# A gated MLP's output projection: float16 weights with scales, and gated rows transposed through DRAM

## The chip, the core and the metric

The kernel runs on one core of a Trainium2 chip. A core has five engines that work side by side, each through its own instructions in order: PE (TensorE, matrix products and transposes, into PSUM), ACT (ScalarE), DVE (VectorE), POOL (GpSimd) and SP (SyncE, which here only issues DMAs). They hand work to each other through semaphores. The metric is the device time of one execution in microseconds (us). The kernel before takes 1732.87 us, median of three runs (1732.65 to 1733.68).

## The reference

A transformer block with pre-normalisation: attention with 32 heads of 16 on 2048 rows of 512, and then a gated MLP whose gate mixes rows.

```python
def _A_ref(x, wqkv, wo):          # 32 heads, Dh = 16
    qkv = (x @ wqkv).reshape(B, S, 3, H, Dh)...
    p = softmax(einsum("bhqd,bhkd->bhqk", q, k) * Dh ** -0.5)
    o = einsum("bhqk,bhkd->bhqd", p, v)
    return o.reshape(B, S, D) @ wo

def _B_ref(x, w_in, w_sp, b_sp, w_out):
    z = gelu(x @ w_in)            # 2048 x 1376
    z1 = z[..., :688]
    z2 = layernorm(z[..., 688:])
    g = einsum("ts,bsf->btf", w_sp, z2) + b_sp[None, :, None]
    return (z1 * g) @ w_out       # 688 -> 512

h = x + _A_ref(layernorm(x), wqkv, wo)
out = h + _B_ref(layernorm(h), w_in, w_sp, b_sp, w_out)
```

Everything is float32 in DRAM. The kernel keeps about float32 accuracy by splitting an operand into a float16 (or float32r) high part and the low part that remains, and by making each product of three: high times high, high times low, low times high (`mm3`, L107 to L110).

## The kernel before

Four stages follow each other. The **projections** (to about 160 us) make q, k and v. **Attention** (to 1296) goes over pairs of key blocks; ACT makes the exponentials, PE scores and weighted sums, DVE maxima. In its shadow POOL does chores: it splits w_sp's quarters, w_in, wo and, last, w_out in six pieces (`out_piece`, through `job`, a planner that deals the chores out by their estimated times), scaled by `out_down` and stored to DRAM as float32r parts (`wu_scr`). Toward the end of attention the first row blocks of its output are fetched (`load_o`), scaled on POOL and split (`split_o`: ACT's cast at L735, DVE's low part at L736) by the iteration numbers n.

The **middle stage** (1296 to 1455) takes 16 row blocks, k = 0 to 15. For a row block PE makes h (`make_h`), transposes the normalised rows (`turn`: PE, a cast on ACT at L99, a low part on DVE at L105), and makes z in four quarters (`make_z`: 12 float16 matmuls of 128x344 into PSUM each, gelu on ACT at L1206). `gate_z` normalises z2, writes z1 to DRAM and forms the sums and differences b11, t1, t2, b22, t3, b21, n4 of the quarters of z2, each cast to float16 (L1210) with a low part (L1211) by `parts`. They feed a Strassen-like product with seven products in the place of eight.

The **final stage** (from 1455.2) runs over p = 0 to 7, a pair of row blocks (p and p + 8) each. `product` (24 float16 matmuls of 128x344, 3.5 us) is called seven times, for b11, t1, t2, b22, t3, b21, n4, into three PSUM banks A, C, B; operands of w_sp's parts come by DMA into a ring of nine (`ask`). ACT evicts p1, q5 and v (L1397, L1402, L1407), DVE adds the four halves right, br, left, bl of the gated rows (L1412 to L1426), POOL multiplies three of them by z1. Between the products of pair p stand the steps of pair p − 1, in a class `Out`: `turn` transposes a gated row block on PE (six 128x128 transposes into PSUM, L1327), `split` casts on ACT (L1335) and takes low parts on DVE (L1336, L1339), `multiply` does 17 float32 matmuls of 128x512 with w_out's parts `wu`, and `store` adds h and writes out (L1357, L1358). `fetch` (L1368) loads z1 and h of the next pair on SP.

The program asks for a manual schedule in the last two stages: every engine issues in the order of the text, and so does SP with its DMAs. Tiles are freed and given out by pools; a tile of a new pool waits for the last access of the closed pools whose memory it takes.

Of the kernel before, what the change touches and what calls it, by code (L numbers as in the profile page):

```python
# [8 lines left out]
F32 = mybir.dt.float32  # L9
# [31 lines left out]
FB = [(i * P, min(P, FH - i * P)) for i in range(6)]  # L41
# [18 lines left out]
def block_kernel(ctx: ExitStack, tc: tile.TileContext, x, wqkv, wo, w_in, w_sp4, b_sp, w_out, out):  # L60
# [30 lines left out]
    wu_scr = [dram.tile([P, 2, D], F32, name=f"wu{i}_scr") for i in range(len(FB))]  # L91
# [640 lines left out]
    def split_o(sb):  # L732
        o = os_.pop(sb)
        o2s[sb] = [e2.tile([P, DB, P], F16, name=f"o2{i}", bufs=1) for i in range(2)]
        nc.scalar.activation(o2s[sb][0], o, AF.Copy, scale=o_up)  # L735
        nc.vector.scalar_tensor_tensor(o2s[sb][1], o, o_up, o2s[sb][0], op0=ALU.mult, op1=ALU.subtract)  # L736
# [47 lines left out]
    with ExitStack() as at:  # L784
# [181 lines left out]
        def out_piece(i):  # L966

            f0, n = FB[i]
            got, load = piece(w_out[f0:f0 + n, :], n)
            t = []  # L970

            def high():
                t.append(wp.tile([P, 2, D], F32R, name="wup", bufs=4)[:n])
                pool.tensor_copy(t[0][:, 0], got[0])

            def low():
                pool.tensor_sub(t[0][:, 1], got[0], t[0][:, 0].bitcast(F32))

            job(load, [(lambda: times(got[0], out_down), TS), (high, CAST), (low, TT)], 12)
            soon(len(chores) + LATER, lambda: nc.sync.dma_start(wu_scr[i][:n], t[0].bitcast(F32)))  # L980

# [69 lines left out]
        for i in range(len(FB)):  # L1051
            out_piece(i)
# [6 lines left out]
        for n in range(0, len(units), 2):  # L1059
# [120 lines left out]
    with ExitStack() as mid:  # L1180
# [28 lines left out]
        def parts(name, k, src, eh, el):  # L1209
            (nc.gpsimd.tensor_copy if eh == "pool" else nc.scalar.copy)(T[name][0][:, k, :], src)  # L1210
            (nc.gpsimd if el == "pool" else nc.vector).tensor_sub(T[name][1][:, k, :], src, T[name][0][:, k, :])  # L1211

        def gate_z(sb, meanwhile):
# [26 lines left out]
            parts("b22", k, b22, "act", el)  # L1240
            nc.gpsimd.tensor_sub(b12, b22, b12)
            parts("t3", k, b12, "pool", "pool")
            parts("b21", k, b21, "act", None)
            e.tensor_sub(t2, b21, t2)
            parts("n4", k, t2, eh, el)

        row = dict(enumerate(h_rows))
        with tc.manual_schedule(engines={E.PE, E.Activation, E.DVE, E.Pool, E.SP}):
# [3 lines left out]
            for k in range(NB):  # L1252
# [38 lines left out]
    with ExitStack() as fin:  # L1291
# [4 lines left out]
        ps_g = fin.enter_context(tc.tile_pool(name="fin_g", bufs=4, space=PSUM))  # L1296
        WB = len(FB) - 1
        TW = P // 2
        fn = FB[-1][1]
# [9 lines left out]
        class Out:  # L1309


            def __init__(self, tb, h, pr):
                self.rows, self.h, self.pr = slice(tb * P, (tb + 1) * P), h, pr
                self.pT = self.acc = None

            def turn(self, *halves):

                if self.pT is None:
                    self.pT = [f2.tile([P, WB + 1, P], F32R, name="pT0"),
                               f2.tile([P, WB, P], F32R, name="pT1")]  # L1320
                    self.tps = {}
                for half in halves:
                    i0 = 3 * half
                    tp = self.tps[half] = ps_t.tile([P, 4, P], F32, name="tp")
                    for i in range(i0, i0 + 3):
                        c = i * P if i < WB else FH - TW
                        nc.tensor.transpose(tp[:, i - i0, :], self.pr[:, c:c + P], ident)  # L1327

            def split(self, *halves):

                hi, lo = self.pT
                for half in halves:
                    i0, tp = 3 * half, self.tps.pop(half)
                    n = 3 - half
                    nc.scalar.activation(hi[:, i0:i0 + 3, :], tp[:, :3, :], AF.Copy)  # L1335
                    nc.vector.tensor_sub(lo[:, i0:i0 + n, :], tp[:, :n, :], hi[:, i0:i0 + n, :].bitcast(F32))  # L1336
                    if half:
                        t = hi[TW:, WB, :]
                        nc.vector.tensor_sub(t, tp[TW:, n, :], t.bitcast(F32))  # L1339

            def multiply(self, blocks, end=True):

                first = self.acc is None
                if first:
                    self.acc = ps_o.tile([P, 512], F32, name="acc")
                hi, lo = self.pT
                for i in blocks:
                    a, z = first and i == blocks[0], end and i == blocks[-1]
                    if i < WB:
                        mm3(self.acc, hi[:, i, :], lo[:, i, :], wu[:, i, 0, :], wu[:, i, 1, :], a, z)  # L1350
                    else:
                        nc.tensor.matmul(self.acc, hi[:, i, :], wu5[0], start=a, stop=False)
# [113 lines left out]
```

## Time and profile before

| | before |
|---|---|
| median of three runs | 1732.87 us |
| profiled execution | 1732.66 us |
| span in its trace | 1730.9 us |
| projections | 0 to about 160 us |
| attention | to about 1296 us |
| middle stage | 1296 to 1455.2 us |
| final stage, seven products of pair 0 | 1455.2 to 1481.5 us |
| loop from there to t3 of pair 7 | 229.2 us |
| from there to the end | 20.2 us |

Rows of a timeline hold start, length, engine, line, operation, what it writes and reads, shapes and types, a count of like instructions in one, and in brackets the idle time before and what ended it. PEld is PE's weight load, which overlaps the matmuls; SPq and ACTq are DMA issues. A row of waits holds the engine, its line and tile, what it waited for, and then us in total, times, and the longest. A row of groups holds a line's operation with count, busy us and mean ns of one, and the idle time before it. The chain of waits is followed back from the last instruction.

### The profile page before, as it was taken

Reading aid. Unit: us, or ns where it says so; the run is one execution under the profiler, and the core shown is the slowest. Engines: PE = TensorE matmul, PEld = TensorE weight load, DVE = VectorE, ACT = ScalarE, POOL = GpSimd, SP = SyncE. Lnnn points to the kernel's source line nnn. Section 1 sums busy time; section 2 is a strip of 40 time slices with the busy share of each in tenths; the row PEclk is TensorE's granted clock in tenths of the full one; section 3 lists DMA queues with packets and bytes.
Section 4 is the critical chain, followed back from the end, with each engine's and each line's share of the span. In section 5 each row is a group of like instructions: output and inputs, shape, how many; then the busy total and the mean of one; then the engine's idle time right before and its main releaser. Section 6 shows DMA issues by size and latency. Waiting matters only on the chain.

```text
span 1730.9 us, 36558 instructions
## 1 busy us (share of the span) xinstructions
PE 1713.6 (99%) x13581; PEld 676.1 (39%) x13581; DVE 1389.4 (80%) x2896; ACT 1301.3 (75%) x2566; POOL 824.8 (48%) x1088
## 2 busy tenths in 40 slices
PE   9999999999999999999999999999999999999999
PEld 4433222222222222222222222222226666777776
DVE  7688999999999999999999999999927776111112
ACT  4334999999999999999999999999995554011000
POOL 1231867776672267877677767600004665100110
PEclk9999999999999999999999999999999999999999
DMA  5534332342231244445345434410125454743440
GB/s 183 162 97 143 101 88 74 98 100 73 75 71 29 63 124 134 139 125 150 92 141 139 133 111 128 108 23 9 45 58 143 131 172 149 274 148 132 171 173 25
DMA packets 185482, 196.13 MB, mean 113 GB/s; under 512 B 65960, under 2 KB 134632, under 8 KB 185304
## 3 DMA queue, kind: packets, MB, share of 16 engines
q1 hardware_dynamic: 183000, 188.16, 37.0%
q10 hardware_dynamic: 2304, 5.64, 0.9%
q8 instruction: 106, 1.74, 0.4%
q14 instruction: 72, 0.59, 0.1%
HBM read 124.92 MB, written 68.75 MB: 112 GB/s over the span
## 4 chain that ended last, share of the span: by engine, by line
PE 72%; DVE 15%; POOL 4%; ACT 3%; DMA 2%; issue 2%; SPq 1%; ACTq 0%; POOLq 0%; DVEq 0%
PE pv L826 24%; PE s L801 16%; PE m L224 9%; DVE mx L229 7%; PE g L108 4%; PE g L110 4%; PE g L109 4%; PE acc L108 3%; PE acc L110 3%; PE acc L109 3%; DMA rc<-r_scr 2%; DVE ab L238 1%; POOL op L1003 1%; ACT pt L810 1%; DVE og L836 1%
## 5 line engine op out<-in xcount | busy, mean ns | idle before, releaser
L810 ACT ACTIVATE pt<-s 128x512 f32<-128x512 f32 x1968 | 1006.9, 638 | 4.7 <-PE m L224 3.6
L229 DVE TENSOR_REDUCE mx<-m 128x1 f32<-128x512 f32 x1510 | 947.2, 682 | 12.8 <-PE m L224 3.9
L801 PE MATMUL s<-qst,kst 50*128 50x512 f16 x2048 | 604.4, 379 | 0.4
L826 PE MATMUL pv<-pt,vst 128*32 128x256 f32 (+1 forms) x6056 | 598.1, 466 | 4.1 <-DVE og L836 0.7
L224 PE MATMUL m<-kst,qst 48*128 48x512 f16 x1510 | 452.3, 381 | 0.0
L801 PEld LDWEIGHTS <-kst 50*128 50x128 f16 x2048 | 131.9, 94 | 352.1 <-issue 322.7
L826 PEld LDWEIGHTS pv<-pt,vst 128*32 128x32 f32 x6056 | 119.5, 108 | 289.9 <-issue 276.6
L224 PEld LDWEIGHTS <-qst 48*128 48x128 f16 x2048 | 159.3, 93 | 173.7 <-issue 123.8
L224 PE MATMUL m<-uvs,qst 48*128 48x512 f16 x504 | 190.7, 380 | 0.0
L238 DVE CUSTOM_DVE_ANT_0 ab<-m,ab 128x512 f32<-128x512 f32 x252 | 170.3, 676 | 2.7 <-ACT ab L234 2.7
L234 ACT ACTIVATE ab<-m 128x512 f32<-128x512 f32 x252 | 157.7, 626 | 16.5 <-PE m L224 15.8
L246 POOL TENSOR_SCALAR nm<-nm 128x16 f32<-128x16 f32 x32 | 6.5, 204 | 331.4 <-DVE nm L243 331.4
L1335 ACT ACTIVATE pT<-tp 128x384 fp32r<-128x384 f32 x32 | 14.0, 488 | 142.0 <-PE tp L1327 142.0
L1413 POOL TENSOR_TENSOR pr<-pr,z 128x344 f32<-128x344 f32 x8 | 7.3, 910 | 193.1 <-DVE pr L1412 181.7
L1003 POOL TENSOR_TENSOR op<-raw,op 128x512 f16<-128x512 f32 x80 | 92.8, 1160 | 5.8
L910 POOL TENSOR_TENSOR raw<-raw 128x512 f32<-128x512 f32 (+1 forms) x84 | 83.1, 989 | 6.7
L915 POOL TENSOR_TENSOR acc_sp<-acc_sp,raw 128x512 f32<-128x512 f32 x63 | 80.4, 1276 | 4.5
L110 PE MATMUL acc<-wi,hT 128*128 128x344 f16 x256 | 79.2, 309 | 2.1 <-DVE hT L105 2.1
L1357 DVE TENSOR_TENSOR y<-acc,h 128x512 f32<-128x512 f32 x16 | 11.1, 691 | 85.9 <-PE acc L1353 84.5
L108 PE MATMUL acc<-wi,hT 128*128 128x344 f16 x256 | 79.1, 309 | 0.0
L109 PE MATMUL acc<-wi,hT 128*128 128x344 f16 x256 | 79.1, 309 | 0.0
L907 POOL TENSOR_SCALAR raw<-raw 128x512 f32<-128x512 f32 (+1 forms) x88 | 52.1, 592 | 19.7 <-DMA raw<-in_wqkv 12.4
(227 smaller groups left out, 2269.3 us busy)
## 6 DMA issues: line engine op xcount, KB each, us to landing
raw<-in_w_sp SPq DMA_DIRECT2D x128, 256.0 KB
s_scr<-op SPq DMA_DIRECT2D x64, 256.0 KB
op<-s_scr SPq DMA_DIRECT2D x32, 512.0 KB
a_scr<-op SPq DMA_DIRECT2D x48, 256.0 KB
op<-a_scr SPq DMA_DIRECT2D x24, 512.0 KB
o_scr<-og SPq DMA_DIRECT2D x64, 128.0 KB
qst<-q_scr SPq DMA_DIRECT2D x192, 32.0 KB
kst<-k_scr SPq DMA_DIRECT2D x48, 128.0 KB
```

Source lines behind the costliest of these rows:

```text
L108: nc.tensor.matmul(ps, lh, rh, start=first, stop=False, **kw)
L109: nc.tensor.matmul(ps, lh, rl, start=False, stop=False, **kw)
L110: nc.tensor.matmul(ps, ll, rh, start=False, stop=last, **kw)
L224: nc.tensor.matmul(acc, q[r, p, c], keys[r, p], start=True, stop=True)
L229: nc.vector.reduce_max(at(t, e if t else e - 1), acc, axis=AX.X)
L234: nc.scalar.activation(ab[0], acc, AF.Abs)
L238: nc.vector.tensor_tensor_reduce(ab[0], acc, ab[0], 0.5, LOW, ALU.add, ALU.max, at(0, 0))
L801: nc.tensor.matmul(s, kst[hg % 2][r, p, kb * P:(kb + 1) * P], qst[hg * NQ + qb][r, p, :], start=True, stop=True)
L810: nc.scalar.activation(pts[p, kb][:, t, :], s, AF.Exp, scale=scales_[hg // 2])
L826: nc.tensor.matmul(pv[0][32 * j:32 * j + 32, a:b], vst[hg % 2][:, c:c + 32], pts[j % 2, kb][:, j // 2, a:b], start=kb == 0, stop=kb == NB - 1,
L910: pool.tensor_mul(got[0] if n else acc, got[0], got[0])
L1003: chores.append((lambda: pool.tensor_sub(t[0][:, 1], of(), t[0][:, 0]), TT))
```

## The change

Weights: w_out is no longer split during attention. In the final stage the raw matrix (`raw_w`, six blocks of 128 rows, the last one zero but for 48 rows, twice) is loaded behind the first fetch. While p = 0, `weigh_w` takes each row's largest magnitude on DVE, and `measure_w` sums them up over a matmul on PE with a matrix `every`, makes a power of two from the largest sum (`powers`), and splits raw_w into two float16 parts, ACT the high one and DVE the low one.

Gated rows: class `Rows` takes the place of `Out`. Each gated row is scaled by a power of two of its own for each half of the columns (`level`, `raise_`); `lower` makes the factor that undoes it, and `gather` applies it when the product of that half is added to h. `multiply` goes over half 1 (8 matmuls a row block) and half 0 (9) into a PSUM accumulator each. For pairs 0 to 6 the rows are transposed in 32x32 squares on DVE (`squares`), written to DRAM (`send`, one DMA) and read back with the squares in their transposed places (`bring`, four DMAs); `hi` and `lo` split what came back. The last pair is transposed on PE (`turn`, `split`).

Borders: `load_o`, its scaling and `split_o` are at other n, with `split_o` on DVE alone. In the middle stage `scale_h` and `minus_mean` come after `turn`, the last `turn` is later by a quarter of z, b21's low part waits for the next k, and n4 is always POOL's; in the last row block POOL makes b22, t3, b21 and n4 and their parts. PSUM for the products is in two pools, `fin_g0` and `fin_g1`, used in turn; h has three buffers.

```diff
-            if n in (476, 480, 504, 508):
-                asked.append(load_o(h_rows[{476: 0, 480: 1, 504: 2, 508: 3}[n]]))
-            if n in (484, 488, 508):
+            if n in (474, 484, 504, 508):
+                asked.append(load_o(h_rows[{474: 0, 484: 1, 504: 2, 508: 3}[n]]))
+            if n in (484, 492, 508):
                 asked.pop(0)()
-            if n in (488, 500, 510):
-                split_o(h_rows[(n - 488) // 11])
+            if len(later) == 1 or n in (498, 510):
+                split_o(h_rows[{498: 1, 510: 2}.get(n, 0)], False)
...
-            parts("b22", k, b22, "act", el)
+            parts("b22", k, b22, "pool" if last else "act", "pool")
             nc.gpsimd.tensor_sub(b12, b22, b12)
             parts("t3", k, b12, "pool", "pool")
-            parts("b21", k, b21, "act", None)
-            e.tensor_sub(t2, b21, t2)
-            parts("n4", k, t2, eh, el)
+            parts("b21", k, b21, "pool" if last else "act", "pool" if last else "later")
+            nc.gpsimd.tensor_sub(t2, b21, t2)
+            parts("n4", k, t2, "pool", "pool")
...
+                new_z(sb)
+                make_z(sb, 1, 0)
+                if k + 1 < NB and k != NB - 2:
+                    turn(row[k + 1])
+                if subs:
+                    subs.pop()(nc.vector)
                 if new is not None:
                     mv, rs = scale_h(new)
                     nb = minus_mean(e2, mv, rs)
-                new_z(sb)
-                make_z(sb, 1, 0)
-                if k + 1 < NB:
+                make_z(sb, 1, 1)
+                if k == NB - 2:
                     turn(row[k + 1])
-                make_z(sb, 1, 1)
...
+        def weigh_w():
+            for i in range(2 * 3):
+                nc.vector.tensor_reduce(w_top[:, i:i + 1], raw_w[:, i, :], axis=AX.X, op=ALU.max,
+                                        apply_absolute_value=True)
+        def measure_w():
+            tp = ps_t.tile([P, 512], F32, name="tp")[:, :2 * 3]
+            nc.tensor.matmul(tp, every, w_top, start=True, stop=True)
+            nc.vector.tensor_reduce(w_low, tp, axis=AX.X, op=ALU.max)
+            powers(w_low, w_up)
+            nc.vector.tensor_scalar(w_down, w_low, 2.0 ** -14, out_down, op0=ALU.mult, op1=ALU.mult)
+            for i in range(2 * 3):
+                nc.scalar.activation(wu[0][:, i, :], raw_w[:, i, :], AF.Copy, scale=w_up)
+                nc.vector.scalar_tensor_tensor(wu[1][:, i, :], raw_w[:, i, :], w_up, wu[0][:, i, :],
+                                               op0=ALU.mult, op1=ALU.subtract)
...
+            def level(self, half, *which):
...
+                nc.vector.tensor_reduce(low, self.pr[:, r, HALVES[half].start:min(HALVES[half].stop, FH)],
+                                        axis=AX.X, op=ALU.max, apply_absolute_value=True)
+                powers(low, up)
...
+            def raise_(self, half, *which):
...
+                    nc.scalar.activation(self.pr[:, w, c], self.pr[:, w, c], AF.Copy,
+                                         scale=self.ups[half, w])
...
+            def send(self, half):
+                nc.sync.dma_start(t_scr[2 * (self.p % 2) + half],
+                                  self.turned[half].rearrange("p q w i a -> p (q w i a)"))
+            def bring(self, half):
+                t = self.turned[half] = f2.tile([P, 4, 2, 3, 32], F32, name="whole")
+                src = t_scr[2 * (self.p % 2) + half].rearrange("(j b) (q c) -> q b j c", j=4, q=4)
+                for q in range(4):
+                    nc.sync.dma_start(t[32 * q:32 * q + 32].rearrange("b j w i a -> b j (w i a)"), src[q])
...
+            raw_w = f1.tile([P, 2 * 3, D], F32, name="raw_w")
...
             nxt = fetch(0)
-            for i in range(WB):
-                nc.sync.dma_start(wu[:, i].bitcast(F32), wu_scr[i])
...
+            nc.sync.dma_start(raw_w[:, :5, :], w_out[:5 * P, :].rearrange("(i p) c -> p i c", p=P))
+            for r0 in (TW - fn, P - fn):
+                nc.sync.dma_start(raw_w[r0:r0 + fn, 5, :], w_out[5 * P:, :])
...
                 product(A, "b11")
+                if p:
+                    before.send(0)
                 nc.scalar.activation(p1, A, AF.Identity, bias=bt)
-                if p:
-                    before[0].multiply(everything)
-                    before[0].store()
                 product(C, "t1")
                 nc.scalar.activation(q5, C, AF.Identity, bias=bb)
                 if p:
-                    before[1].turn(0, 1)
-                    before[1].split(0, 1)
+                    before.bring(0)
+                    before.hi(1)
+                    before.lo(1)
+                    before.lower(1, 0, 1)
+                    accs = [before.multiply(1, w) for w in range(2)]
+                else:
+                    weigh_w()
                 product(A, "t2", False)
                 nc.scalar.activation(v, A, AF.Identity, bias=bt)
                 if p:
-                    before[1].multiply(everything)
-                    before[1].store()
+                    for w in range(2):
+                        before.gather(1, w, accs[w])
+                else:
+                    measure_w()
                 product(C, "b22", False)
                 nc.vector.tensor_add(right, C, v)
                 nc.gpsimd.tensor_mul(right, right, z1t[:, FC:])
-                nc.gpsimd.tensor_copy(top.pr[:, FH:], top.pr[:, FH - TW:FH])
+                if p:
+                    before.hi(0)
+                    before.lo(0)
+                    before.lower(0, 0, 1)
+                    accs = [before.multiply(0, w) for w in range(2)]
                 product(A, "t3", False)
                 nc.vector.tensor_add(br, A, q5)
-                nc.gpsimd.tensor_mul(br, br, z1b[:, FC:])
-                nc.gpsimd.tensor_copy(bot.pr[:, FH:], bot.pr[:, FH - TW:FH])
+                (nc.vector if last else nc.gpsimd).tensor_mul(br, br, z1b[:, FC:])
+                now.level(1, 0, 1)
+                now.raise_(1, 0, 1)
+                if p:
+                    for w in range(2):
+                        before.gather(0, w, accs[w])
+                        before.store(w)
+                if not last:
+                    now.squares(1)
                 product(B, "b21")
+                if last:
+                    for w in range(2):
+                        now.turn(1, w)
+                        now.split(1, w)
+                else:
+                    now.send(1)
                 nc.vector.tensor_add(left, B, p1)
                 (nc.vector if last else nc.gpsimd).tensor_mul(left, left, z1t[:, :FC])
...
                 product(A, "n4", False)
+                if not last:
+                    now.bring(1)
                 nc.vector.scalar_tensor_tensor(bl, A, bb, z1b[:, :FC], op0=ALU.add, op1=ALU.mult)
...
+                    now.level(0, 0, 1)
+                    now.raise_(0, 0, 1)
+                    now.squares(0)
+            now.turn(0, 0)
+            now.split(0, 0)
...
+            accs = [now.multiply(1, w) for w in range(2)]
...
+            now.turn(0, 1)
+            now.split(0, 1)
+            acc = now.multiply(0, 0)
+            now.gather(0, 0, acc)
+            now.store(0)
+            acc = now.multiply(0, 1)
+            for c in (slice(0, D // 2), slice(D // 2, D)):
+                now.gather(0, 1, acc, c)
+                now.store(1, c)
```

More of the change, by code (lines that the diff above doesn't have):

```diff
@@ L40 @@
 PAIR = "s0 M0 join s2 M4 M1 s1 H s3 invert M2 s5 M3 H out M5 s4 M7 turn s6 s7 M6 P".split()
-FB = [(i * P, min(P, FH - i * P)) for i in range(6)]
+HF = 3 * P
 FC = FH // 2
@@ L964, in split_piece @@
             job(load, steps, 12)
[L966 to L980, printed above, removed]
         def quarters(p, c):
@@ L1307, in product @@
             ask()
[L1309 to L1350, printed above, removed]
-                    else:
-                        nc.tensor.matmul(self.acc, hi[:, i, :], wu5[0], start=a, stop=False)
-                        nc.tensor.matmul(self.acc, hi[:, i, :], wu5[1], start=False, stop=z)
-            def store(self):
-                y = f2.tile([P, D], F32, name="y")
-                nc.vector.tensor_add(y, self.acc, self.h)
-                nc.sync.dma_start(out[self.rows, :], y)
@@ L1422, in block_kernel @@
                 if last:
-                    bot.turn(1)
-                    bot.split(1)
+                    now.level(0, 0)
+                    now.raise_(0, 0)
                 product(A, "n4", False)
+                if not last:
+                    now.bring(1)
                 nc.vector.scalar_tensor_tensor(bl, A, bb, z1b[:, :FC], op0=ALU.add, op1=ALU.mult)
-                top.turn(0, 1)
-                top.split(0, 1)
-            bot.multiply(range(3, WB + 1), False)
-            top.multiply(range(3), False)
-            bot.turn(0)
-            bot.split(0)
-            top.multiply(range(3, WB + 1))
-            bot.multiply(range(3))
-            top.store()
-            bot.store()
+                if last:
+                    now.level(0, 1)
+                    now.raise_(0, 1)
+                else:
+                    now.level(0, 0, 1)
[3 more added lines that the diff above has]
+            now.split(0, 0)
+            now.lower(1, 0, 1)
+            now.lower(0, 0, 1)
+            accs = [now.multiply(1, w) for w in range(2)]
+            for w in range(2):
+                now.gather(1, w, accs[w])
+            now.turn(0, 1)
[7 more added lines that the diff above has]
+                now.store(1, c)
 def kernel(**inputs):
```

137 lines of the change are left out of this document (113 added, 24 removed).

## The prediction

> **What bounds the kernel now.** I read the page first, then the windows by stage, the waits at the two stage borders, and the timeline of those borders and of the last steps. A windows row holds the span, then busy time and instructions of PE, PEld, DVE, ACT and POOL, the granted clock, the DMA share and GB/s.
>
> ```profile
> PE 1713.6 (99%) x13581; PEld 676.1 (39%) x13581; DVE 1389.4 (80%) x2896; ACT 1301.3 (75%) x2566; POOL 824.8 (48%) x1088
> ```
>
> ```profile
> 1250.00:1296.00 46.00, 45.07 (x312) 9.37 (x309) 9.56 (x25) 44.17 (x53) 3.18 (x5) 1.00 0.22 53
> 1296.00:1455.20 159.20, 156.74 (x999) 97.65 (x996) 124.56 (x403) 82.69 (x144) 96.81 (x114) 1.00 0.47 145
> ...
> 1467.36:1481.50 14.14, 14.14 (x100) 9.58 (x98) 1.55 (x3) 0.55 (x1) 3.21 (x5) 1.00 1.03 362
> 1481.50:1710.70 229.20, 229.20 (x1451) 162.83 (x1449) 40.09 (x82) 22.92 (x49) 20.36 (x32) 1.00 0.43 156
> ```
>
> The end of attention (1250 to 1296) is ACT's. The middle stage is PE's but for 2.5 us. The loop (1481.5 to 1710.7) is PE's wholly: whatever goes from PE there is gained, whatever makes PE wait is lost. The other engines are mostly idle in it, DVE 189 of 229 us.
>
> **Attention.** The removed out-piece chores ran on POOL, which is far from busy at the end; I cost them at nothing. Two casts of o leave ACT for DVE; each took ACT's time up to the next row:
>
> ```profile
> 1250.65 0.77 ACT L735 ACTIVATE o<-o,fig 128x512 f16<-128x512 f32 x1
> 1251.27 4.08 ACT L810 ACTIVATE pt<-s 128x512 f32<-128x512 f32 x8
> ...
> 1274.71 0.72 ACT L735 ACTIVATE o<-o,fig 128x512 f16<-128x512 f32 x1
> 1275.32 1.02 ACT L819 ACTIVATE pt<-s 128x1024 f32<-128x1024 f32 x1
> ```
>
> 0.62 + 0.61 = **−1.2**, covered on DVE, 36 of 46 us idle. The border into the middle stage: **−0.2**, an estimate (0 to −1).
>
> **Middle stage.** The turn and its low part move ahead of DVE's small operations, which removes PE's wait for hT:
>
> ```profile
> PE acc L110 <- DVE hT L105: 2.1, 6, 0.4
> ```
>
> 2.1, plus 0.1 for each of the six in the matmul pipeline, is **−2.65**; 0 if another wait takes its place.
>
> **Border to the final stage.** The last row block now puts t3, b22, b21 and n4 on POOL, one after another. POOL's pitch, and the start of its chain before:
>
> ```profile
> 1448.00 0.84 POOL L1211 TENSOR_TENSOR b<-z,b 128x344 f16<-128x344 f32 x1
> 1448.80 0.92 POOL L1241 TENSOR_TENSOR z<-z,z 128x344 f32<-128x344 f32 x1
> 1449.78 0.47 POOL L1210 CAST t<-z 128x344 f16<-128x344 f32 x1
> 1450.33 0.83 POOL L1211 TENSOR_TENSOR t<-z,t 128x344 f16<-128x344 f32 x1
> ...
> 1457.85 0.91 POOL L1241 TENSOR_TENSOR z<-z,z 128x344 f32<-128x344 f32 x1 [1.14 <-ACT z L1222]
> ```
>
> 0.80 for a low part, 0.98 for a subtraction, 0.55 for a cast: 4 × 0.55 + 4 × 0.80 + 2 × 0.98 = 7.4, so POOL ends at 1465.25. The final stage's tiles lie where the middle stage's lay: its first eviction and fetch both came just after DVE's last operation there.
>
> ```profile
> 1463.26 0.55 ACT L1397 ACTIVATE p<-g,fig 128x344 f32<-128x344 f32 x1 [0.71 <-DVE n L1211]
> 1463.56 0.79 SPq L1368 DMA_DIRECT2D z<-z_scr  x2
> 1463.85 0.31 PE L108 MATMUL g<-t,op 128*128 128x344 f16 x1 [0.56 <-ACT p L1397]
> ...
> 1465.35 3.60 SPq L1380 DMA_DIRECT2D wu<-wu_scr  x5
> ...
> 1471.67 1.62 SPq L1368 DMA_DIRECT2D z<-z_scr  x2
> ```
>
> So p1, released 0.16 after POOL's end, slips 2.15 us, to about 1465.4, and t2 starts at 1466.0 instead of 1463.85. The fetch goes out at about 1465.7, and raw_w behind it on SP's queue. In the old run the next fetch went out at 1471.67, and I take that its lane came free when the first wu had landed, eight DMAs earlier: 1.73 MB in 8.1 us, which at the 362 GB/s of the window from 1467.36 is 4.8 of transfer and 3.3 of start. The fetch of 1.2 MB and raw_w's 1.31 MB then land at 1465.7 + 3.3 + 7.0 = 1476.0. Now PE's queue has measure_w's matmul between t2 and b22, and it needs six reductions of 128x512 on DVE; the nearest row:
>
> ```profile
> L353 DVE TENSOR_REDUCE most<-wg 128x1 f32<-128x512 f32 x8 | 5.1, 677 | 0.3 <-DMA wg<-in_wqkv 0.3
> ```
>
> At a pitch of 0.64 they end at 1479.8, b22 starts at 1480.0 instead of 1467.36: **+12.6**. Bounds: +8 if the fetch isn't held by POOL (4.7 earlier), +16 if the second fetch's 1.2 MB share the queues.
>
> **PE after the idle time.** PE idles some 10 us there. The kernel's own first matmuls were slower than the ones that followed:
>
> ```profile
> 1.19 8.23 PE L527 MATMUL acc<-idle 128*128 128x512 bf16 x30 [1.19 <-DVE idle L521]
> 13.25 3.62 PE L511 MATMUL acc<-wv,xT 128*128 128x512 f16 x16
> ```
>
> From the second, (3.62 − 0.38) / 15 = 0.216 us a matmul; 29 such and 0.38 make 6.64, and 8.23 were needed: **+1.6** for a cold start, 0 if that slowness was the kernel start's alone (the granted clock reads 1.00 throughout). The Trainium skill, "TensorE: Matmul & The Clock Gate", section "Part 1: The HAM clock gate (the "warmup" mystery)", says that PE falls back to half clock after some 3.4 us idle and leaves it after as long busy, which costs 1.7; the clock column speaks against it with its 1.00 in every window, the first matmuls' spacing for it. By the rule the sum would be 1750.8, by the column 1749.1. No row here shows a stop of that length in mid-kernel.
>
> **Loop, what PE saves.** In the old order each row block is transposed on PE and multiplied in float32:
>
> ```profile
> 1695.59 0.82 PE L1327 MATMUL tp<-ident,pr 128*128 128x128 f32 x6
> 1696.24 0.31 PE L108 MATMUL g<-t,op 128*128 128x344 f16 x1
> ...
> 1699.62 0.51 PE L108 MATMUL acc<-wu,pT 128*128 128x512 f32 x1
> 1699.97 0.39 PE L109 MATMUL acc<-wu,pT 128*128 128x512 f32 x1
> ...
> 1703.48 0.39 PE L1353 MATMUL acc<-wu,pT 128*128 128x512 f32 x1
> ```
>
> Transposes: 0.65 × 14 = 9.1. The second to the last of a row block's 17 matmuls stand (1703.48 − 1699.97) / 15 = 0.234 apart, in float16 0.216: 34 × 7 × 0.018 = 4.3. First float32 matmul 0.35 instead of 0.23: 14 × 0.12 = 1.7. **−15.1.**
>
> **Loop, what PE now waits for.** Two row blocks' transposes stood between products; nothing does now. Each multiply needs its split straight behind a product's eviction:
>
> ```profile
> 1695.44 0.31 PE L110 MATMUL g<-t,op 128*128 128x344 f16 x1
> 1695.79 0.55 ACT L1402 ACTIVATE q<-g,fig 128x344 f32<-128x344 f32 x1 [6.93 <-PE g L110]
> 1696.23 0.86 ACT L1335 ACTIVATE pT<-tp 128x384 fp32r<-128x384 f32 x2
> ...
> L1222 ACT ACTIVATE z<-z,nb,rs_u 128x688 f32<-128x688 f32 x16 | 15.4, 961 | 43.4 <-DVE nb L764 38.9 <-DMA o<-o_scr 4.5
> L1211 DVE TENSOR_TENSOR b<-z,b 128x344 f16<-128x344 f32 x9 | 4.5, 514 | 15.5 <-ACT b L1210 15.5
> ```
>
> Half 1: PE has multiply(1) right behind t1, but its hi (128x768) is behind q5 on ACT: 0.35 until q5 starts, 0.44 for it, 0.95 for hi (961 ns at 688 elements gives 1.07, half the pair-row above 0.43 × 2 = 0.86), 0.05, less a matmul's 0.146 spacing: **1.64**. Half 0: hi(0) is ready, lo(0) stands behind the addition of right on DVE: 0.35 + 0.52 + 0.93 (514 ns at 344, doubled less the fixed part) + 0.05, less the first two matmuls, which need only hi (2 × 0.216 and 0.146 of pipeline, 0.58): **1.27**. (1.64 + 1.27) × 7 = **+20.4**; bounds 0 (were a planner to put them earlier; the order is by hand) and 26 with the longer hi and two separate fixed parts.
>
> The round trip of half 1 counts from the end of t3. br's addition on DVE takes 0.35 + 0.52, its product on POOL 0.91, the reduction over 608 elements 0.8 (677 ns at 512), three small operations that make a power of two 0.5 (an estimate), two raises on ACT 1.0 (0.55 at 344), five hops between engines 0.3: 4.4. The 32x32 transposes of 640 elements have no row of their size; at 514 ns for 344 they take 1.0, at three times that 3. So they end 5.4 to 7.4 after t3, and I take 6.2, nearer the first, which is measured on the same engine with the same count. Legs through DRAM, from the chain of waits:
>
> ```profile
> 764.63 4.25 DMA s_scr<-op
> ...
> 1301.61 5.30 DMA rc<-r_scr
> 1308.16 3.13 DMA rc<-r_scr
> ```
>
> 6.2 + 4.25 + three more issues of 0.45 + 3.13 = 14.9; due at 14.65 (four products of 3.51 and q5): 0.3 late, 7 times: **+2**, nothing if either leg is shorter. Half 0's trip has 6 us to spare. The other new work on DVE (reductions, scales, transposes, four scaled additions in the place of two, some 12 us a pair by like rows, 7 pairs 84 us) runs where 189 us were idle, and nothing on PE is behind it but lo, which is counted: nothing; were it in front of right's addition it would cost what it lasts.
>
> **Tail.** DVE's addition behind the last t3, 0.2 after PE's end, and the last addition of y:
>
> ```profile
> 1710.92 0.52 DVE L1416 TENSOR_TENSOR pr<-g,q 128x344 f32<-128x344 f32 x1 [2.88 <-PE g L110]
> ...
> 1727.16 0.69 DVE L1357 TENSOR_TENSOR y<-acc,h 128x512 f32<-128x512 f32 x1 [1.40 <-PE acc L110]
> ```
>
> From 1710.7 to the span's end, 1730.9, are 20.2. Now PE has 7.0 of products, 1.3 of transposes, 34 × 0.216 = 7.3 of matmuls; two waits for raised rows, 0.3 and 0.7; gather in halves 1.1; the store, as before, 1730.9 − 1727.85 = 3.05: 20.8, **+0.6**.
>
> **Sum**, against the profiled execution's own 1732.66 (span 1730.9; 0.2 under the median): −1.2 − 0.2 − 2.65 + 12.6 + 1.6 − 15.1 + 20.4 + 2 + 0.6 = +18.05: **1750.7**.
>
> **Rivals.**
> A, faster: the waits are covered. Condition: raw_w has landed and is reduced before t2 ends, and hi and lo start before the products in front of them end. Then −1.2 − 0.2 − 2.65 − 0.6 (t2's old wait for p1) − 15.1 + 0.6 = −19.15, 1713.5. For it: DVE, ACT and POOL are idle four fifths of the loop. Against: the program order. Chance 0.08.
> B, no change: only the border is covered, loop stalls stay: A's sum and the 20.4, 1733.9. For it: raw_w's queue has nothing but the fetch ahead. Against: the fetch itself waits, as the old run's did. Chance 0.08.
> C, late round trip: legs of 4.25 and 5.30 make 17.1, 2.45 late, 7 × = 17 instead of 2: 1766. It decides from legs of 7.1 together. For it: the queue carried 362 GB/s when bunched; against: 43% on average. Chance 0.17.
> D, loop stalls of half the size (hi at 0.80, lo started under right's addition) or a border of +8: 1738 to 1743. Chance 0.12.
> E, a lock between DVE and POOL. A DVE operation with two inputs beside a POOL operation took far longer than its like alone:
>
> ```profile
> 1457.87 1.26 DVE L1238 TENSOR_TENSOR t<-z,z 128x344 f32<-128x344 f32 x1 [1.10 <-ACT z L1222]
> 1461.53 0.50 DVE L1244 TENSOR_TENSOR t<-z,t 128x344 f32<-128x344 f32 x1
> ```
>
> lo(0) beside POOL's product for right would cost 0.76 × 7 = 5.3: 1756. That is if POOL starts first; lo(0) is behind right's addition with no hop, so DVE does. Chance 0.05. The Trainium skill, "SBUF — State Buffer", section "Who interferes with whom", says the same: the first to issue holds the shared pair, the other waits. The row agrees.
>
> **How the numbers follow.** The forecast holds 0.50, from 1744 to 1758. The range, 1733 to 1768, leaves out A and C's far part. A measurement here tells about 0.2%, 3.5 us, from no change: faster 0.12 (A, and half of B, whose 1733.9 has a spread of its own), same 0.07 (the rest of B and the foot of D), slower 0.81.
>
> **What would show it.** Border: PE idle near 10 us before b22, ended by the w_top reductions; raw_w landing near 1476. Loop: PE waiting 1.5 to 1.7 for hi of half 1 behind each t1 and 1.2 to 1.3 for lo of half 0 behind each b22; no transposes until the last pair. Round trip: that hi waiting for a DMA instead of q5 means C. The middle stage without a PE wait for hT. Wrong: PE near 100% in the loop (A), or a p1 that doesn't wait for POOL.

## The result, and the profile after

The changed kernel takes 1760.57 us, median of four runs (1757.43 to 1767.72), against 1732.99 (1732.65 to 1733.68): a ratio of 1.0162, interval 1.015 to 1.0175, slower by 27.6 us. Forecast were 18 (1750.7). The execution whose profile follows is the longest of the four, 1767.72 with a span of 1765.9; the one of before had 1730.9, so it is 35.0 us that the trace has to account for. Of all executions reported below, a single one, in the second experiment, took 5488.76 us; ratios and intervals leave it out.

Windows of the changed kernel, columns as before (span, busy time of PE, PEld, DVE, ACT, POOL, granted clock, DMA share, GB/s): middle stage, border, the first products behind it, loop, tail.

```profile
1296.00:1455.20 159.20, 156.51 (x1001) 98.37 (x999) 125.59 (x403) 81.54 (x144) 97.33 (x114) 1.00 0.48 145
1455.20:1480.50 25.30, 13.05 (x70) 7.81 (x68) 6.09 (x13) 2.97 (x5) 8.34 (x12) 0.75 0.60 201
1480.50:1485.00 4.50, 4.50 (x17) 2.40 (x18) 3.52 (x10) 3.53 (x6) 0.00 (x0) 0.50 0.76 300
1485.00:1744.30 259.30, 235.50 (x1448) 140.47 (x1447) 87.44 (x204) 37.63 (x64) 22.97 (x23) 0.98 0.54 173
1744.30:1766.00 21.70, 16.24 (x96) 9.15 (x93) 13.25 (x34) 3.96 (x8) 0.47 (x2) 0.98 0.14 49
```

Three things stand in it. The middle stage has 2.7 us of idle PE, and 2.5 before: nothing gained. In the border PE idles half the time, and the granted clock, 1.00 in every window of before, is 0.50 behind it. And the loop, in which PE was never idle before, has 23.8 us of idle PE.

PE's waits of the changed kernel, first in the middle stage and then from the border to the last t3 (what waited, for what; us in total, times, longest):

```profile
PE acc L108 <- ACT hT L99: 1.4, 1, 1.4
PE tp L1176 <- ACT hn L1269: 1.0, 5, 0.2
PE acc L110 <- DVE hT L105: 0.3, 1, 0.3
```

```profile
PE acc L108 <- ACT pT L1398: 18.6, 11, 3.4
PE tp L1327 <- issue: 7.9, 1, 7.9
PE acc L110 <- DVE pT L1407: 5.2, 6, 1.1
```

The 18.6 are multiplies that wait for `hi` (`pT`, ACT), the 5.2 those that wait for `lo` of half 0 (`pT`, DVE), and the 7.9 stand ahead of the measuring matmul, which needs raw_w's reductions. Waits for `hi` were forecast for half 1 alone, seven times; here they are eleven.

The border, from the timelines of POOL, ACT, SP, DVE and PE:

```profile
1464.45 0.83 POOL L1196 TENSOR_TENSOR n<-t,n 128x344 f16<-128x344 f32 x1
1465.31 0.80 SPq L1465 DMA_DIRECT2D z<-z_scr  x2
1465.32 0.55 ACT L1492 ACTIVATE p<-g,fig 128x344 f32<-128x344 f32 x1 [6.45 <-POOL n L1196]
1465.91 0.45 PE L108 MATMUL g<-t,op 128*128 128x344 f16 x1 [4.39 <-ACT p L1492]
1467.10 0.43 SPq L1475 DMA_DIRECT2D raw_w<-in_w_out  x1
1476.36 3.65 DVE L1321 TENSOR_REDUCE w<-raw_w 128x1 f32<-128x512 f32 x6 [16.94 <-DMA raw_w<-in_w_out]
1480.11 0.56 PE L1327 MATMUL tp<-w,every 128*128 128x6 f32 x2 [7.86 <-issue]
1480.53 0.45 PE L108 MATMUL g<-b,op 128*128 128x344 f16 x1
1480.77 0.49 PE L109 MATMUL g<-b,op 128*128 128x344 f16 x1
```

POOL's last operation ends at 1465.28 (its start and its length). The fetch and p1 follow it at once, raw_w's load goes out behind the fetch and lands before 1476.36, the reductions end at 1480.01, and b22 starts at 1480.53. Its first 16 matmuls are 0.24 to 0.29 us apart, where 0.146 is usual.

### The profile page after: what moved, and what is told of

It reads as the page before. It is cut to its first block, busy times and chain, and to the rows that moved or that the text cites. A ratio compares the mean times of both kernels' runs of the same rounds, so it can differ in the third digit from the quotient of the medians.

```text
span 1765.9 us, 36677 instructions
## 1 busy us (share of the span) xinstructions
PE 1713.9 (97%) x13499; PEld 645.4 (37%) x13499; DVE 1450.7 (82%) x3051; ACT 1317.7 (75%) x2584; POOL 813.5 (46%) x1062
## 4 chain that ended last, share of the span: by engine, by line
PE 70%; DVE 15%; DMA 6%; POOL 2%; issue 2%; ACT 2%; SPq 2%; ACTq 0%; DVEq 0%; POOLq 0%
PE pv L829 25%; PE s L804 17%; PE m L224 9%; DVE mx L229 7%; PE acc L108 3%; PE acc L110 3%; PE acc L109 3%; PE g L108 3%; PE g L110 3%; PE g L109 3%; DMA t_scr<-squares 2%; DMA rc<-r_scr 2%; DVE ab L238 1%; DVE og L839 1%; DVE rs_t L125 1%
## 5 line engine op out<-in xcount | busy, mean ns | idle before, releaser
L229 DVE TENSOR_REDUCE mx<-m 128x1 f32<-128x512 f32 x1510 | 947.8, 683 | 12.6 <-PE m L224 3.9
L1361 ACT ACTIVATE pr<-pr,up 128x304 f32<-128x304 f32 (+1 forms) x32 | 17.0, 574 | 138.8 <-DVE up L1315 138.8
L108 PE MATMUL g<-t,op 128*128 128x344 f16 x192 | 60.6, 316 | 4.4 <-ACT p L1492 4.4
```

The source lines that it names most:

```text
L108: nc.tensor.matmul(ps, lh, rh, start=first, stop=False, **kw)
L229: nc.vector.reduce_max(at(t, e if t else e - 1), acc, axis=AX.X)
```

## The experiments

**The load of raw_w ahead of the fetch.**

```diff
-            nc.gpsimd.memset(raw_w[:, 2 * 3 - 1, :], 0.0)
-            nxt = fetch(0)
+            nc.vector.memset(raw_w[:, 2 * 3 - 1, :], 0.0)
             nc.sync.dma_start(raw_w[:, :5, :], ...)
...
+            nxt = fetch(0)
```

> The changed kernel with the load of raw_w ahead of the first fetch on SP's queue, and its last block zeroed by DVE instead of POOL. Theory (the border wait is raw_w landing behind the fetch): the reductions end before t2 does, b22 starts near 1472.3 in place of 1480.53 and runs at full speed, so 8.2 + 2.2 = 10.4 us less, about 1750. Rival (POOL's chain of the last row block is what holds the border): p1 still starts at 1465.3 and less than 3 us are gained, about 1758.

1751.08 us (1749.74 to 1754.41), ratio 1.0109, interval 1.0093 to 1.0126: 9.5 less. Timelines of this kernel, SP and PE:

```profile
1442.74 0.38 SPq L1474 DMA_DIRECT2D raw_w<-in_w_out  x1
...
1467.34 0.82 SPq L1465 DMA_DIRECT2D z<-z_scr  x2
```

```profile
1467.95 0.45 PE L108 MATMUL g<-t,op 128*128 128x344 f16 x1 [5.84 <-ACT p L1492]
...
1473.24 0.28 PE L1327 MATMUL tp<-w,every 128*128 128x6 f32 x2
```

The load goes out in the middle stage, and the measuring matmul stands right behind t2. b22 starts at 1473.38, 7.2 us earlier, and runs at full speed. What is left is t2's own wait for p1, 5.84 us, and t2 at half speed behind it. That wait is 1.4 longer than in the changed kernel: raw_w's reductions now stand among DVE's operations for the last row block, and POOL's chain ends at 1467.31 instead of 1465.28. So raw_w behind the fetch cost 9.5 us; that POOL's chain holds p1 is tried further down, with p1 in other memory.

**The multiplies one product later.** PE's order alone: half 1's multiply behind t2, half 0's behind t3.

```diff
                     before.lower(1, 0, 1)
-                    accs = [before.multiply(1, w) for w in range(2)]
...
                 product(A, "t2", False)
                 nc.scalar.activation(v, A, AF.Identity, bias=bt)
                 if p:
+                    accs = [before.multiply(1, w) for w in range(2)]
...
                     before.lower(0, 0, 1)
-                    accs = [before.multiply(0, w) for w in range(2)]
                 product(A, "t3", False)
+                if p:
+                    accs = [before.multiply(0, w) for w in range(2)]
```

> The changed kernel with the multiply of half 1 behind product t2 on PE (it stood ahead of it) and that of half 0 behind t3. Nothing else moves. Theory (the loop's waits are a product's eviction and a split in front of a multiply, so 3.5 us of other product cover them): PE's waits of 13.2 us for half 1 and 13.7 for half 0 go, and with them 4.3 us of slow matmuls, about 1731. Rival (the waits are the round trip through DRAM, and come back at the new place): half 0 keeps what is over 1.28 in each pair, 4 to 5 us, and 1740 or more.

The 13.2 and 13.7 are counted from start to start of the matmuls, beyond their usual distance. Measured: 1736.94 us (nine executions from 1735.76 to 1739.01, and the one named above), ratio 1.0023, interval 1.0013 to 1.0033: 23.6 less. All that is left of PE's waits from 1485 to 1730 is this row of the kernel's waits:

```profile
PE tp L1423 <- ACT pr L1361: 1.2, 1, 1.2
```

No wait for `hi` or `lo` came back at the new place, so 3.5 us of product cover them, late trips through DRAM included. The 31 were read from the profile of the longest execution. The same loop in the profile of the first experiment holds 12.7 us of waits for half 1, 9.3 for half 0 and 1.65 of slow matmuls, 23.6 in all, which is what this experiment gained.

**The fetch behind the trip of half 0.**

```diff
-                nxt = None if last else fetch(p + 1)
+                nxt = fetch(1) if not p else None
...
                     before.bring(0)
+                    nxt = None if last else fetch(p + 1)
```

> The changed kernel with the fetch of the next pair issued behind bring of half 0; it stood ahead of send of half 0. Theory (half 0 comes late in some pairs because its send stands behind 1.2 MB of fetch): its waits fall to 1.28 in each pair, 9.0 in all instead of 13.7, and the slow matmuls behind them go, 1752 to 1756; the wait for half 1 stays at 1.6. Rival (the trip itself is that slow): waits of 1.8 to 3.6 stay, 1759 to 1762.

1758.61 us (1756.55 to 1760.37), between what theory and rival gave; the interval of the ratio, 1.0127 to 1.0161, overlaps the changed kernel's. The time doesn't tell; the traces do. The chain of waits of the changed kernel, in a pair in which half 0 came late, and SP's rows of the same pair in this kernel, `send` (t_scr) and `bring` (whole):

```profile
1539.01 9.79 DMA t_scr<-squares
...
1550.17 2.86 DMA whole<-t_scr
1553.19 0.85 ACT pT L1398
1554.09 0.61 PE acc L108
```

```profile
1538.49 0.38 SPq L1384 DMA_DIRECT2D t_scr<-squares  x1
...
1543.54 1.74 SPq L1392 DMA_DIRECT2D whole<-t_scr  x4
1545.38 0.85 SPq L1465 DMA_DIRECT2D z<-z_scr  x2
```

Behind the fetch the send took 9.79 us; ahead of it `bring`, which needs it, went out 5.05 us after it. That pair is the worst, but all six pairs with a fetch go the same way: from the issue of half 0's send to that of its `bring` pass 6.3 to 9.9 us in the changed kernel's trace, 6.7 to 7.3 in the first experiment's, which has the same order, and 4.6 to 5.7 here. PE's waits of this kernel in the loop:

```profile
PE acc L108 <- ACT pT L1398: 11.3, 7, 2.4
PE acc L110 <- DVE pT L1407: 7.8, 7, 1.1
```

Seven and seven: half 0 no longer waits for `hi` in any pair, and waits for `lo` in each; the longest for `hi`, 2.4, is a late trip of half 1. That is the forecast's loop, and 19.1 us where the changed kernel's profile has 23.8. The first experiment's trace sets a bound to what this is worth: there, with trips of about 7 us, half 0 waited 9.3 us, only 0.3 more than seven times 1.28.

**All of it, and p1 in memory that is free early** (`e4_all` in the texts further down). The three edits above, and this one:

```diff
-                p1, v, q5 = [f2.tile([P, FC], F32, name=n) for n in ("p1", "v", "q5")]
+                p1, v, q5 = [f1.tile([P, FC], F32, name=n, bufs=2) for n in ("p1", "v", "q5")]
```

> The three edits together, and p1, v and q5 in the pool fin_1, whose memory is free before the middle stage ends, so that p1 doesn't wait for POOL's last operation. Theory (each wait was a matter of order): −10.4 − 4.4 (the wait before t2) − 31 from 1760.6, 1715; faster than the kernel before by 1%. Rival (something else becomes the bound, the DMA queue or DVE): 1725 or more, with a new wait on PE in the loop.

1719.81 us (1718.18 to 1720.06), ratio 0.9921, interval 0.9905 to 0.9938: faster than the kernel before. Its window from b22 of the first pair to the end of the last b21:

```profile
1466.34:1700.60 234.26, 233.48 (x1489) 145.16 (x1488) 95.44 (x221) 42.46 (x72) 26.21 (x28) 1.00 0.65 213
```

PE idles 0.8 us in it, and no wait of t2 for p1 is left in the trace. 1715 was expected from the long profile's 31 us; with 23.6 it is 1722.

**PE busy while it waits.** The changed kernel, and products into a tile that nobody reads, `stay_busy(30)` ahead of t2 and `stay_busy(72)` ahead of `measure_w`.

```diff
+        def stay_busy(n):
+            tp = ps_t.tile([P, 512], F32, name="tp")
+            for _ in range(n):
+                nc.tensor.matmul(tp[:, :FC], T["b11"][0][:, 0, :P], T["b11"][0][:, 0, :], start=True, stop=True)
...
                     weigh_w()
+                    stay_busy(30)
...
+                    stay_busy(72)
                     measure_w()
```

> The changed kernel, and PE does products that nobody reads while it waits in the border: 30 matmuls of 128x344 ahead of t2 and 72 ahead of the measuring matmul. Theory (b22 and t2 run at half speed because PE had stood still): both products take 3.35 us, the clock stays 1.00, and b22 ends 2.2 us earlier, 1758 in all. Rival (the operands or the queue made them slow): 0.286 between matmuls as in the changed kernel, and no gain.

1759.63 us (1756.88 to 1763.77), too wide to tell 1 or 2 us. Windows over t2 and over b22:

```profile
1466.39:1469.80 3.41, 3.41 (x24) 2.30 (x24) 0.00 (x0) 0.39 (x1) 0.00 (x0) 1.00 0.89 279
1481.70:1485.20 3.50, 3.50 (x26) 2.39 (x27) 2.43 (x8) 2.44 (x4) 0.00 (x0) 1.00 0.90 352
```

Both products run at full clock, and DMA moves as much as beside the slow b22 (352 GB/s, there 300). So the slowness came from PE's standing still, and not from the operands or the queue. b22 ends 0.9 us earlier and not 2.2, because in this run the reductions of raw_w started 1.5 us later.

**The middle stage, three kernels.** First the combined kernel with the last `turn` in its usual place (`e5_turn_usual`):

```diff
-                if k + 1 < NB and k != NB - 2:
+                if k + 1 < NB:
                     turn(row[k + 1])
...
-                if k == NB - 2:
-                    turn(row[k + 1])
```

> e4_all with the last turn of the middle stage in its usual place, ahead of the second quarter of z, also at k = 14. Theory (the change's later turn made the wait of 1.56 + 0.42 us for hT of the last row block): both go, the middle stage is 2.0 us shorter, 1717.8. Rival (hT of that block is late wherever the turn stands): the same 1719.8, with a wait of PE at k = 15.

1719.78 us (1719.08 to 1720.11): nothing gained. The wait for hT is gone, but the wait for hn, the normalised rows that `turn` transposes, has grown from 1.6 to 2.4 us. It is the longest of PE's waits in this stage:

```profile
PE tp L1176 <- ACT hn L1267: 2.4, 6, 1.3
```

Then, from that kernel, `scale_h` and `minus_mean` back ahead of `turn`, as in the kernel before (`e6_mid_before`):

```diff
+                if new is not None:
+                    mv, rs = scale_h(new)
+                    nb = minus_mean(e2, mv, rs)
                 new_z(sb)
                 make_z(sb, 1, 0)
                 if k + 1 < NB:
                     turn(row[k + 1])
                 if subs:
                     subs.pop()(nc.vector)
-                if new is not None:
-                    mv, rs = scale_h(new)
-                    nb = minus_mean(e2, mv, rs)
```

> e5_turn_usual with scale_h and minus_mean ahead of turn again, so the middle stage's order is the old one but for b21's late low part. Theory (the change traded PE's wait for the low part of hT, 5 x 0.53, for a wait of the transposes for hn, 5 x 0.4): the waits for hT come back, those for hn go, the middle stage is 0.6 longer than in e5, 1718.4. Rival (the new order does gain what was forecast, and something else lost it): 2.65 longer, 1720.5.

1714.50 us (1714.06 to 1715.23), ratio 0.9894, interval 0.9878 to 0.9911: neither theory nor rival. It is 5.3 us faster than the kernel without the edit. With the old order of the small operations the middle stage, from its first transpose to z's last matmul, takes 155.53 us instead of 159.28, and no wait for hT or hn is left; most of the rest are two waits behind it that shrink, t2's for p1 (0.8, now none) and the first multiply's (1.0, now 0.2). So the wait for hT was not due to those small operations. To settle it, the kernel before with b21's low part made late, and nothing else (`parts` keeps the operation in a list `subs`):

```diff
+            if el == "later":
+                subs.append(sub)
...
-            parts("b21", k, b21, "act", None)
+            parts("b21", k, b21, "act", None if last else "later")
...
                     turn(row[k + 1])
+                if subs:
+                    subs.pop()(nc.vector)
                 make_z(sb, 1, 1)
```

> The kernel before with one edit: b21's low part on DVE waits for the next row block and stands behind its turn; scale_h and minus_mean stay where they were. Theory (that low part is what made the low part of hT late, so this edit alone takes the waits of 5 x 0.53 + 0.44 away, as in e6): 3.1 to 3.9 us less, 1729 to 1730. Rival (the small operations of scale_h ahead of turn are the cause, and e6 gained through what the change does elsewhere): no gain, 1733.

1728.20 us (1728.06 to 1728.76), ratio 0.9972, interval 0.9962 to 0.9983: 4.8 less than the kernel before, and more than the theory's 3.1 to 3.9. Its window over the middle stage, and that of the kernel before over the same work:

```profile
1295.92:1451.58 155.66, 155.31 (x1002) 98.84 (x1000) 123.17 (x407) 83.92 (x144) 98.78 (x116) 1.00 0.50 148
```

```profile
1295.57:1455.04 159.47, 157.01 (x1003) 98.08 (x1000) 124.87 (x403) 82.69 (x144) 96.65 (x114) 1.00 0.47 145
```

3.8 of the 4.8 us lie here. The old wait of t2 for p1, 0.6, has gone as well.

**The tail.** In the last pair, the low parts of half 1 behind the scaling that the next transposes wait for. `split` is cut in two for it:

```diff
                         now.turn(1, w)
-                        now.split(1, w)
+                        now.split_hi(1, w)
...
                     now.raise_(0, 0)
+                    for w in range(2):
+                        now.split_lo(1, w)
```

> e5_turn_usual, and in the last pair the low parts of half 1 behind the scaling of the first row block's half 0 on DVE. Theory (the first transposes behind n4 wait 1.37 us for that scaling): the wait goes, 1716.5. Rival (it moves to the multiply of half 1, which needs those low parts): 1717.8, as e5.

> e6_mid_before, with the low parts of the last pair's half 1 behind the scaling of the first row block's half 0, as in e8. Theory (in e8 0.74 of the 1.37 us were kept): 1713.8. Rival (nothing is kept, since half 0's own low part is next): 1714.5.

1719.01 us (1718.36 to 1719.70) and 1714.01 us (1713.25 to 1714.56, ratio 0.989, interval 0.9874 to 0.9907). Against the kernels without it, 1719.78 and 1714.50, that is 0.8 and 0.5, less than the spread of the runs, so no gain is shown. (The first text's 1717.8 was the time expected of `e5_turn_usual`, not the measured one.) In the traces the wait moved in part, in both kernels: the row of the kernel without the edit, and of the one with it, whose last multiply waits for DVE's `gather` into h.

```profile
PE tp L1421 <- ACT pr L1359: 1.2, 1, 1.2
```

```profile
PE acc L108 <- DVE h L1455: 0.5, 1, 0.5
```

1714.01 is the lowest median, 1.1% under the kernel before, but not to be told from 1714.50.

## Why the prediction was right, and where its sizes were off

The direction, the place and the cause of both large losses were as forecast. The time is in the range, but 2.6 us above the stretch from 1744 to 1758 to which the forecast itself gave 0.50. The terms, against the profile of the changed kernel (start to start, in us):

| term | forecast | profile |
|---|---|---|
| attention and its border | −1.4 | −1.0 |
| middle stage | −2.65 | +0.2 |
| border, b22's start | +12.6 | +14.0 |
| b22 at low clock | +1.6 | +2.2 |
| PE's savings in the loop | −15.1 | −13.0 |
| loop waits, round trip and low clock among them | +22.4 | +31.2 |
| tail | +0.6 | +1.4 |
| sum | +18.05 | +35.0 |

This is the longest execution. With the loop waits of the first experiment's profile, 23.6, in the place of 31.2 the column sums to 27.4, and the medians differ by 27.6. That is an estimate, since the two kernels differ in the border, but it tells where a usual execution lost the missing 9.4: 2.9 in the middle stage, 2.1 in PE's savings, 1.4 in the border, 1.2 in the loop and 1.8 in the other three. Every term came out higher than forecast, so the direction doesn't rest on errors that cancel.

**Border.** Each time of its chain was met: POOL's end 1465.25 and 1465.28, t2 1466.0 and 1465.91, the reductions' end 1479.8 and 1480.01, b22 1480.0 and 1480.53. POOL's end was met with some luck: its chain began at 1457.51 instead of 1457.85 and took 7.8 us instead of 7.4. The term is larger because PE came to the border 0.8 us earlier, and because b22 started 0.5 later. The experiment that moved raw_w shows the one link; that no wait for p1 is left where p1 was moved shows the other.

**b22 at low clock.** The term stood on one row of the kernel's own start, against a clock column of 1.00; the keep-busy run shows that the choice was right. The 2.2 us are what 16 matmuls lost (0.286 instead of 0.146). The granted clock is 0.50, half, as the Trainium skill, "TensorE: Matmul & The Clock Gate", section "Part 1: The HAM clock gate (the "warmup" mystery)", has it. t2 ran at half speed too, which cost nothing, since PE had to wait for raw_w behind it anyway.

**Loop waits.** The 1.64 and 1.27 of the forecast were measured as 1.53 to 1.59 and 1.28 in the pairs without a late trip (half 1 once took 1.87, where q5 started 0.3 later). `hi` and `lo` of 768 elements were taken as 0.95 and 0.93. `hi` took 0.84; the mean of `lo` is 1.06, but six of the seven took 0.95 to 0.96 and one 1.66, of which more under the rivals. Their rows in the groups from 1485 to 1745 (count, busy us, mean ns, idle time before):

```profile
L1398 ACT ACTIVATE pT<-whole 128x768 f16<-128x768 f32 x14 | 11.7, 838 | 17.5 <-DMA whole<-t_scr 17.5
L1407 DVE TENSOR_TENSOR pT<-whole,pT 128x768 f16<-128x768 f32 x7 | 7.4, 1055 | 4.0 <-ACT pT L1398 4.0
```

Half 1's trip came late in two pairs and cost 1.9 us beyond 1.59 a pair. The forecast had +2 for it, as 0.3 in each of seven pairs, so the size was met by luck.

What failed is the sentence "Half 0's trip has 6 us to spare". It left out that half 0's send stands in SP's queue behind the fetch of 1.2 MB and an operand: the send took 9.79 us in the worst pair, and `bring` went out at least 6.3 us behind it in each pair with a fetch, where 4.25 was the row. Rival C was thus right in mechanism, but mostly for the other half: beyond 1.28 a pair, half 0 waited 4.7 us more (13.7 − 7 × 1.28), about half of the 8.8 that are missing here. The rest, 4.3, are matmuls at half clock behind waits, which no part of the forecast had. Both are sizes of the longest execution; in the first experiment's they are 0.3 and 1.65. The third experiment shows the first; the second shows that neither matters once the multiplies have a product in front of them.

**PE's savings.** The first float32 matmul's 0.35 was no extra: it starts 0.03 behind the last matmul of the product ahead of it, so the pair's 33.8 us of before are just 24.5 + 1.3 + 34 × 0.234. That took 1.7 of the 2.1.

**Middle stage.** "The turn and its low part move ahead of DVE's small operations, which removes PE's wait for hT": five of the six waits did go, but by the other edit in the same place. b21's low part alone, made late, takes 4.8 us from the kernel before. The moved small operations make hn late and cost the middle stage 3.75 (159.28 against 155.53), and the last row block, whose `turn` is later, still waits 1.4 and 0.3 for hT. So the bound "0 if another wait takes its place" is what came. (2.1 and six times 0.1 are 2.7, not 2.65.)

**Rivals.** A and B fell with PE's idle time in loop and border. D's price for the border, +8, didn't occur, as the fetch did wait for POOL. E's lock would make `lo` of half 0 take 1.69 (0.93 + 0.76). In four pairs `lo` started ahead of POOL's product for right, as the prediction argued, and took 0.95 or 0.96; it was POOL's product, begun beside it, that took 1.50 to 1.55 instead of 0.91. In two pairs POOL's product was all but over when `lo` started. In the pair from 1643, where half 0 came late, POOL started 0.06 us ahead of `lo`. One of the four, and then that pair:

```profile
1516.47 0.95 DVE L1407 TENSOR_TENSOR pT<-whole,pT 128x768 f16<-128x768 f32 x1
1516.63 1.55 POOL L1512 TENSOR_TENSOR pr<-pr,z 128x344 f32<-128x344 f32 x1 [20.42 <-DVE pr L1511]
...
1663.61 0.91 POOL L1512 TENSOR_TENSOR pr<-pr,z 128x344 f32<-128x344 f32 x1 [20.10 <-DMA whole<-t_scr]
1663.67 1.66 DVE L1407 TENSOR_TENSOR pT<-whole,pT 128x768 f16<-128x768 f32 x1 [0.20 <-ACT pT L1398]
```

So E's mechanism is there, and the one that starts second pays. It hit `lo` once in seven pairs and made it 0.7 us longer, which is in the 4.7 above.

By the medians, raw_w's place is worth 9.5 us and the multiplies' 23.6; what the combined kernel gained besides, 7.7 (1760.57 − 33.1 − 1719.81), is left for p1's memory and the fetch's place, which were not told apart. These are 40.8 together. Without them the change is 13.2 faster than the kernel before, and 40.8 − 13.2 are the 27.6 lost.

## What to carry to other kernels

An eviction and a split in front of a matmul need another product ahead of them in PE's order: the same operations, one place later, gave back 23.6 us, the largest part of the 40.8 that order and place had cost. Load what is ready before what has to wait: that was worth 9.5. A small transfer that somebody waits for belongs ahead of the large one in the queue; the traces show it arrive earlier, though the time alone didn't tell. Where an edit moves two things in one place, try each alone: here one was worth 4.8 us and the other took it back.

## What was not expected of the hardware

PE's clock fell after waits shorter than the one in the border, and shorter than the 3.4 us of the rule in the prediction. Windows of the first experiment's kernel, a wait of 2.5 us and what followed 1 us behind it:

```profile
1563.80:1566.30 2.50, 0.22 (x3) 0.03 (x2) 0.05 (x1) 1.39 (x2) 0.00 (x0) 1.00 0.89 254
1567.10:1570.60 3.50, 3.50 (x11) 1.18 (x9) 1.44 (x4) 0.00 (x0) 0.00 (x0) 0.52 0.90 265
```

From 1567.18 on eight matmuls ran at half clock, 0.43 us apart instead of 0.22, and 1.65 us were lost. In the changed kernel's profile a wait of 2.8 us at 1578.4 had no such sequel:

```profile
1578.40:1581.40 3.00, 0.39 (x4) 0.10 (x2) 0.12 (x1) 1.39 (x2) 0.00 (x0) 1.00 0.91 279
1581.40:1586.00 4.60, 4.60 (x25) 2.21 (x25) 2.90 (x7) 0.00 (x0) 0.00 (x0) 1.00 0.95 272
```

Two shorter waits had it. In the changed kernel's pair from 1643 PE waited 1.0 us for `hi` and, after two matmuls, 1.25 for `lo`, and what followed 0.7 us later ran at half clock, 1.6 us lost:

```profile
1666.10:1669.50 3.40, 3.40 (x10) 1.25 (x9) 0.00 (x0) 0.00 (x0) 0.00 (x0) 0.52 0.20 80
```

So a wait of 1 to 3 us costs its length and, sometimes, some 1.7 us more; no run here tells what decides it. Four executions of the changed kernel lay 10.3 us apart, and four of the fastest kernel, which has one wait of that size in its loop, 1.3. That the half clock makes the difference is not shown, as the late trips vary between executions too.
